# First expert layer on 256 columns of x with the weights held, for pairs of tiles of one expert

## The chip, the cores and the metric

The kernel runs on one core of a Trainium2 chip. The metric is the device time of one execution in microseconds. Engines work side by side, each through its own instructions in order: TensorE (PE in the profile, its weight loads PEld), VectorE (DVE), ScalarE (ACT), GpSimd (POOL) and SyncE (SP), which issues transfers. PSUM is the memory that TensorE writes; SBUF holds everything else.

## What is computed

Chunked attention gives x, 4608 rows (8 x 576) of 512 numbers. Each row is then sent to one of eight experts, and the expert's two layers give the output row:

```python
out = np.matmul(attn, v_c)                     # chunks of 64 rows; scores with max and exp before
x = out.transpose(0, 2, 1, 3).reshape(B, S, H * D)
logits = np.einsum('bsd,de->bse', x, w_gate)
local_gate = 1.0 / (1.0 + np.exp(-np.einsum('bsd,de->bse', x, w_local).squeeze(-1)))
for b in range(B):
    prev_e = -1
    for s in range(S):
        fresh_e = int(np.argmax(logits[b, s]))
        if s == 0 or local_gate[b, s] < 0.5:
            e = fresh_e
        else:
            e = prev_e if prev_e >= 0 else fresh_e
        prev_e = e
        ...
        h = np.maximum(x[b, s] @ w1[e], 0.0)
        out[b, s] = p[e] * (h @ w2[e])
```

w1[e] is 512 x 1024, w2[e] is 1024 x 512. The experts get very different numbers of rows, and which row goes where is known only on the chip.

## The kernel before, in words

The first 200 us are attention and routing; the rest is the expert loop. The routed rows are sorted by expert in half tiles of 64 rows. Two half tiles make a tile of 128 rows; there are 46 tile places and 38 tiles in use. A tile whose halves have two experts is *mixed*. Tiles 0 to 2 are worked beside the end of attention, by an order written out by hand (the table `PAR["drain"]`: `x0` is the transposes of tile 0's x, `m0` its first layer, `h0` the splitting of its h, `y0` its second layer, `g` a gather). From tile 3 (`EARLY`) on, `step(t, ok, mix)` writes one tile; from tile 36 (`TMIN`) on it also asks whether the tile is in use. All this stands under a manual schedule: each engine keeps the order of the code.

Products are made in three passes, since each operand is split in a high part and a low part (the number format fp32r): high by high, high by low, low by high (`PASSES`). `mm1` is the first layer: x stationary, 512 columns of W1 moving, 24 matmuls a tile, into h with the rows on partitions. So h has to be transposed for the second layer: ScalarE's Relu brings it to `hsb` (L680), eight TensorE transposes (L588) put it into PSUM again, ScalarE casts the high part (L590) and VectorE subtracts for the low part (L591). `mm2` is the second layer, 24 matmuls; `emit_y` scales by the probability and scatters the rows by an indirect transfer on GpSimd.

Order in `step(t)`, on each engine: first layer of t (L627), its probabilities (`probs`, on VectorE with one exponential on ScalarE) and Relu; the gather of tile t + 2 (L594); `next_x(t + 1)`: four transposes of x with cast and low part; `refill(0, t)`; second layer of t - 1 (L641) and its output (L699, L700); `refill(1, t - 1)`; transposes and parts of h of tile t.

`refill(which, t)` loads nothing unless the expert changes behind tile t (a register from `regs`). Then it splits the raw weights that wait in SBUF into the parts that the matmuls read, four chunks: ScalarE casts all four (L96), the low parts (L97) go to VectorE for chunks 0, 2 and 3 and to GpSimd for chunk 1; then SyncE fetches the next expert's raw weights (L868 for W1, L871 for W2). W1 must not be overwritten before the last first layer that reads it is through.

A mixed tile takes its upper 64 rows from the raw weights of the next expert, in plain fp32 (`mm1_upper` L635, `mm2_upper` L647); `rejoin` on GpSimd adds high and low parts for that. `either` is the branch between both forms; a branch is decided on each engine by a register that it has loaded.

The buffers that matter: h stands in one PSUM tile of two banks (`new_h`), y in one (`new_y`), and three PSUM tiles `tr` serve all transposes. `slots` works out the row numbers of the tiles from 8 on; its pieces stand in the first steps of the loop.

Of the kernel before, what the change touches and what calls it, by code (L numbers as in the profile page):

```python
# [24 lines left out]
P = 128  # L25
# [26 lines left out]
    ),  # L52
    "p0": "AVPA",
# [12 lines left out]
def tile_attention_then_moe(ctx: ExitStack, tc, q, k, v, wg, wl, w1, w2, out):  # L66
# [557 lines left out]
    def mm1(xs, hs, c):  # L624
        for n, (a, w) in enumerate(PASSES):
            for j in range(2):
                nc.tensor.matmul(hs[:, j], xs[a][:, c], W1[w][c][:, 512 * j:512 * j + 512],  # L627
                                 start=(c == 0 and n == 0), stop=(c == 3 and n == 2))

    def mm1_upper(xf, hm):
        for c in range(4):
            for j in range(2):
                nc.tensor.matmul(hm[HT * j:HT * j + HT], xf[:, c], raw1[c][:, 512 * j:512 * j + 512],  # L635
                                 start=(c == 0), stop=(c == 3))

    def mm2(hx, y, c):
        for f in (2 * c, 2 * c + 1):
            for n, (a, w) in enumerate(PASSES):  # L640
                nc.tensor.matmul(y, hx[f // 4][a][:, f % 4], W2[w][c][:, f % 2, :],  # L641
                                 start=(f == 0 and n == 0), stop=(f == 7 and n == 2))
# [28 lines left out]
    def new_m():  # L671
        return ps_l.tile([P, 512], F32, name="m", tag="lg")
# [130 lines left out]
    def gather_full(t):  # L803
        xgs[t] = gather(t, pc.tile([P, XR], F32, name="xg", bufs=4), x_d)
# [1 line left out]

    te8 = pc.tile([P, NTILE, E], F32, name="te8", bufs=1)
    tb8 = pc.tile([1, NTILE, E], F32, name="tb8", bufs=1)
    regs = pc.tile([1, 4, NTILE], I32, name="regs", bufs=1)
# [69 lines left out]
    @contextmanager  # L879
    def when(v):  # L880
        if v is None:
            yield
        else:
            with tc.If(v != 0):  # L884
                yield

    def step(t, ok, mix):
        tail = t >= TMIN
        if t < NTILE:
            hs, hsb = new_h()  # L890
            hm = new_m()
            with when(ok[t]):
                plain = lambda: [mm1(xps[t], hs, c) for c in range(4)]
                either(mix[t], plain, lambda: (plain(), mm1_upper(full[0, t], hm)))
# [4 lines left out]
        if t + 2 < NTILE:  # L899
            ok[t + 2] = oks[t + 2] if t + 2 in oks else valid(t + 2)  # L900
            with when(ok[t + 1]):
                gather_full(t + 2)
        if t + 1 < NTILE:
            next_x(t + 1, mix)
        y, ym = (new_y(), new_m()) if t > EARLY else (None, None)

        def down(cs):
            def plain():
                for c in cs:
                    mm2(hps[t - 1], y, c)  # L910

            either(mix[t - 1], plain, lambda: (plain(), mm2_upper(full[1, t - 1], ym) if cs[-1] == 3 else None))
            if cs[-1] == 3:
                emit_y(t - 1, y, prc[t - 1], mix[t - 1], ym)

        def next_h(g):
            hps.setdefault(t, []).append(h_parts(hsb, g, tail and t != TMIN + 2))

        if tail and t < NTILE:
            with tc.If(ok[t] != 0) as cmp:  # L920
                down((0, 1))
                next_h(0)
                down((2, 3))
            with cmp.Else():
                with when(ok[t - 1]):
                    down((0, 1, 2, 3))
        elif t > EARLY:
            with when(ok[t - 1]):
                down((0, 1, 2, 3))
        if t < NTILE:  # L930
            refill(1, t - 1)
            with when(ok[t]):
# [4 lines left out]
    def next_x(t, mix):  # L937
        mix[t] = mixs[t] if t in mixs else mixed(t)
        if EARLY < t <= TMIN:
            xps[t] = x_parts(xgs[t], t == TMIN)  # L940
        full[0, t] = rejoin(mix[t], *xps[t], "x")
        refill(0, t - 1)

    def valid(t):
        return reg(2, t, 1, [ET.PE, ET.Activation, ET.DVE, ET.Pool, ET.SP]) if t >= TMIN else None

    with tc.manual_schedule(engines=MAN | {ET.SP, ET.Pool}):
        mix, ok = {}, {EARLY: None, EARLY + 1: None}
        oks, mixs = {}, {}
        next_x(EARLY, mix)  # L950
        for t in range(EARLY, TMIN + 3):
            step(t, ok, mix)
            n = t - EARLY
            if 20 <= t < 26:
                oks[t + 16] = valid(t + 16)
                mixs[t + 16] = mixed(t + 16)
            run(sl[n:n + 1])
        with when(ok[TMIN + 2]):
            for t in range(TMIN + 3, NTILE + 1):
                step(t, ok, mix)  # L960

# [20 lines left out]
```

## Time and profile before

| | |
|---|---|
| time, median of 3 runs | 727.39 us (725.78 to 731.74) |
| profiled execution | 728.72 us, span of its instructions 726.9 us |
| tiles in use | 38 (38 scatters of y) |
| VectorE, ScalarE, GpSimd busy | 50%, 37%, 26% of the span |
| weight reloads in the loop | 28 of W1 chunks, 28 of W2 chunks (seven changes of expert) |
| DMA queues | 42.1% and 8.2% of 16 engines' span |

A row of a timeline gives the start in us, the length in us, engine, line, operation, out<-in and the number of instructions merged; in brackets how long the engine was idle before and what ended it. Matmuls are pipelined: the length of one covers its way through the array, and the next starts earlier, so rates are read from starts. A row of a group gives the count, then busy time and mean length in ns, then idle time before. In the rows of the 40 slices a digit is the busy share in tenths.

### The profile page before, as it was taken

The page shows a single profiled execution, that of the slowest core. Times are in us where ns is not written, and L with a number is a line of the kernel's source. Part 1 is how long each engine was busy: PE and PEld are TensorE (multiplying, and loading weights), DVE is VectorE, ACT ScalarE, POOL GpSimd, SP SyncE. Part 2 cuts the span into 40 slices and gives each one's busy share as a digit, 9 for nine tenths or more (in the row PEclk, how much of TensorE's full clock was granted, in tenths as well). Part 3 has the DMA queues.
Part 4 walks back from the last instruction along what each step waited for, and adds up shares of the span by engine and source line. Part 5 has one row for each costly group of instructions (what it writes and reads, how often), then busy time and mean ns, then how long its engine had stood idle before and what let it go on. Part 6 is the DMA issues. An engine that isn't in the chain of part 4 may idle for free. (4 is left out here: it accounts for less than half of the span.)

```text
span 726.9 us, 17103 instructions
## 1 busy us (share of the span) xinstructions
PE 661.4 (91%) x5594; PEld 524.8 (72%) x5594; DVE 362.0 (50%) x852; ACT 272.2 (37%) x432; POOL 188.1 (26%) x230
## 2 busy tenths in 40 slices
PE   4779898777999999999999999999999999999971
PEld 4668676565777788777888887778877888777861
DVE  2547655574685585256232562572576323454310
ACT  3547665554521234341222443422454222432210
POOL 3322233345022132123121231331243212231100
PEclk9989999998999999999999999999999999999986
DMA  9999999996833144145111253441277111333100
GB/s 211 201 200 234 233 240 245 247 254 178 217 102 118 46 148 135 71 146 164 42 46 46 84 164 101 148 156 47 79 239 249 60 44 46 97 111 130 49 19 15
DMA packets 102928, 97.49 MB, mean 134 GB/s; under 512 B 42672, under 2 KB 79536, under 8 KB 102768
## 3 DMA queue, kind: packets, MB, share of 16 engines
q1 hardware_dynamic: 96608, 75.70, 42.1%
q0 software_dynamic: 6160, 19.85, 8.2%
q8 instruction: 78, 1.28, 0.8%
q14 instruction: 82, 0.67, 0.3%
HBM read 76.48 MB, written 19.56 MB: 132 GB/s over the span
## 5 line engine op out<-in xcount | busy, mean ns | idle before, releaser
L641 PE MATMUL y<-w2h,hp 128*128 128x512 f32 x608 | 203.7, 405 | 10.3 <-DVE hp L591 6.3
L627 PE MATMUL h<-w1h,xp 128*128 128x512 f32 x608 | 178.3, 403 | 0.0
L641 PEld LDWEIGHTS y<-w2h,hp 128*128 128x128 f32 x608 | 114.9, 190 | 39.1 <-DVE hp L591 8.9
L627 PEld LDWEIGHTS h<-w1h,xp 128*128 128x128 f32 x608 | 111.4, 189 | 23.9 <-ACTq L863 0.2
L641 PE MATMUL y<-w2l,hp 128*128 128x512 f32 x304 | 121.1, 399 | 0.0
L700 POOL DMA_INDIRECT out<-ysb,sidx x38 | 41.2, 1085 | 273.5 <-DVEq L863 197.4
L627 PE MATMUL h<-w1l,xp 128*128 128x512 f32 x304 | 95.9, 396 | 0.0
L590 ACT CAST hp<-tr 128x512 fp32r<-128x512 f32 x76 | 41.2, 589 | 108.0 <-PE tr L588 97.0
L591 DVE TENSOR_TENSOR xp<-tr,xp 128x512 fp32r<-128x512 f32 x39 | 27.0, 691 | 106.5 <-ACTq L863 67.0
L699 DVE TENSOR_SCALAR ysb<-y,ppr 128x512 f32<-128x512 f32 x35 | 26.2, 747 | 92.7 <-PE y L641 81.7
L627 PEld LDWEIGHTS h<-w1l,xp 128*128 128x128 f32 x304 | 57.0, 188 | 14.7 <-DVEq L863 0.7
L641 PEld LDWEIGHTS y<-w2l,hp 128*128 128x128 f32 x304 | 57.9, 190 | 12.3
L680 ACT ACTIVATE hsb<-h 128x1024 f32<-128x1024 f32 x35 | 35.9, 1027 | 67.5 <-PE h L627 64.9
L591 DVE TENSOR_TENSOR hp<-tr,hp 128x512 fp32r<-128x512 f32 x76 | 49.2, 685 | 13.5 <-ACT hp L590 12.5
L613 ACT ACTIVATE pex<-pex 128x8 f32<-128x8 f32 x38 | 7.9, 209 | 117.2 <-DVE pex L612 117.2
L594 POOL DMA_INDIRECT xg<-x_d,gidx x36 | 36.9, 1026 | 40.7 <-issue 19.3
L97 POOL TENSOR_TENSOR w1l<-raw,w1h 128x512 fp32r<-128x512 f32 (+1 forms) x15 | 27.7, 1844 | 70.6 <-ACT w1h L96 70.6
L242 PE MATMUL o<-v,pT 64*64 64x65 f32 x1152 | 32.0, 235 | 13.5 <-DMA v<-in_v 12.9
L242 PEld LDWEIGHTS o<-v,pT 64*64 64x64 f32 x1152 | 24.6, 143 | 23.0 <-DMA v<-in_v 15.8
L588 PE MATMUL tr<-ident,hsb 128*128 128x128 f32 x304 | 40.3, 273 | 0.3 <-ACT hsb L680 0.3
L97 DVE TENSOR_TENSOR w2l<-raw,w2h 128x1024 fp32r<-128x1024 f32 x21 | 39.9, 1952 | 0.9 <-issue 0.9
L588 PEld LDWEIGHTS tr<-ident,hsb 128*128 128x128 f32 x304 | 35.3, 141 | 6.8 <-ACT w2h L96 1.2
(173 smaller groups left out, 832.5 us busy)
## 6 DMA issues: line engine op xcount, KB each, us to landing
raw<-in_moe_w SPq DMA_DIRECT2D x72, 512.0 KB, 5.0
x_d<-xs SPq DMA_DIRECT2D x18, 521.0 KB, 5.7
v<-in_v SPq DMA_DIRECT2D x72, 128.0 KB, 6.0
qt<-in_q SPq DMA_DIRECT2D x11, 512.0 KB, 6.4
kt<-in_k SPq DMA_DIRECT2D x11, 512.0 KB, 7.6
qt<-in_q SPq DMA_DIRECT2D x6, 256.0 KB, 6.2
kt<-in_k SPq DMA_DIRECT2D x6, 256.0 KB, 6.7
qt<-in_q SPq DMA_DIRECT2D x4, 384.0 KB, 7.0
```

What stands on the lines that cost most here:

```text
L97: (lo_eng or nc.vector).tensor_tensor(lo, raw, hi.bitcast(F32), ALU.subtract)
L242: nc.tensor.matmul(o[64 * cp:64 * cp + 64, cc, DV * h:DV * h + D + 1], pT[64 * cc:64 * cc + 64, 4 * j + h, 64 * cp:64 * cp + 64], vt[64 * ...
L588: nc.tensor.transpose(ps[:, n], src_of(n), ident)
L590: return [tr, lambda: nc.scalar.copy(hi, box["ps"]), lambda: V.tensor_tensor(lo, box["ps"], hi.bitcast(F32), ALU.subtract)]
L591: lambda: V.tensor_tensor(lo, box["ps"], hi.bitcast(F32), ALU.subtract)]
L594: nc.gpsimd.indirect_dma_start(out=dst, out_offset=None, in_=src, in_offset=bass.IndirectOffsetOnAxis(ap=gidx[t].bitcast(U32), axis=0))
L613: lambda: nc.scalar.activation(ex[:, 0], ex[:, 0], AF.Exp),
L627: nc.tensor.matmul(hs[:, j], xs[a][:, c], W1[w][c][:, 512 * j:512 * j + 512], start=(c == 0 and n == 0), stop=(c == 3 and n == 2))
L641: nc.tensor.matmul(y, hx[f // 4][a][:, f % 4], W2[w][c][:, f % 2, :], start=(f == 0 and n == 0), stop=(f == 7 and n == 2))
L680: nc.scalar.activation(hsb, hs.rearrange("p j f -> p (j f)"), AF.Relu)
L699: either(mix, lambda: V.tensor_scalar(ysb, y, pr, None, ALU.mult), lambda: y_mixed(ysb, y, ym, pr))
L700: nc.gpsimd.indirect_dma_start(out=out, out_offset=bass.IndirectOffsetOnAxis(ap=sidx[t].bitcast(U32), axis=0), in_=ysb, in_offset=None, bo ...
```

## The change

In the loop the tiles 4 to 35 are taken in 16 pairs (4, 5), (6, 7) and so on, by a new function `pair`. A new register, made by one more VectorE compare, says whether the first half of tile t and the second half of tile t + 1 have the same expert; since the halves are sorted, all four then have it.

If they have, the first layer is `mm1_pair`: blocks of 128 x 128 of W1 are stationary and x of both tiles moves, 256 columns, so that h comes out with its features on partitions. It is called twice, for features 0 to 511 and 512 to 1023, 48 matmuls each. ScalarE's Relu writes the high part straight from PSUM and VectorE the low part (`relu_pair`); the transposes of h, `hsb` and both casts are left out. Otherwise both tiles are worked as before, inside the pair's order. The second layer is the same.

The order in `pair(t)`: first layer of t (or features 0 to 511 of both tiles), second layer of t - 1, transposes and parts of h of t if the tiles are single; `refill(0, t)`; first layer of t + 1 (or the other features of both), gathers for the pair after the next, x of the next two tiles with `refill(0, t + 1)` behind it; second layer of t, parts of h of t + 1 if single. The high and low parts of x of both tiles lie in `xhi` and `xlo`, those of h in three buffers taken in turn (`SLOTS`), which attention used before. Three tiles instead of two are gathered in the drain.

```diff
+    def mm1_pair(xs, hT, g):
+        for f in range(4):
+            for c in range(4):
+                for n, (a, w) in enumerate(PASSES):
+                    nc.tensor.matmul(hT[:, f], W1[w][c][:, P * (4 * g + f):P * (4 * g + f) + P], xs[a][:, c],
+                                     start=(c == 0 and n == 0), stop=(c == 3 and n == 2))
+    def relu_pair(hp, hT):
+        nc.scalar.activation(hp[0], hT, AF.Relu)
+        V.scalar_tensor_tensor(hp[1], hT, 0.0, hp[0].bitcast(F32), ALU.max, ALU.subtract)
...
-        lambda: V.tensor_tensor(regs[:, 3], te[0:1, 0:NTILE], tb, ALU.not_equal),
+        lambda: (V.tensor_tensor(regs[:, 3], te[0:1, 0:NTILE], tb, ALU.not_equal),
+                 V.tensor_tensor(regs[:, 4, 0:NTILE - 1], te[0:1, 0:NTILE - 1], tb[:, 1:NTILE], ALU.is_equal)),
...
-        g=lambda: [lambda t=t: gather_full(t) for t in (EARLY, EARLY + 1)],
+        g=lambda: [lambda t=t: gather_full(t) for t in (EARLY, EARLY + 1, EARLY + 2)],
...
+    def next_xs(t, mix):
+        xp2[t] = (pc.tile([P, 4, 256], F32R, name="xhi", tag="xp", bufs=1),
+                  pa2.tile([P, 4, 256], F32R, name="xlo", tag="xs", bufs=3))
+        for d in range(2):
+            xps[t + d] = [x[:, :, P * d:P * d + P] for x in xp2[t]]
+            hilo(lambda n, d=d: xgs[t + d][:, P * n:P * n + P], *xps[t + d])
+            mix[t + d] = mixs[t + d] if t + d in mixs else mixed(t + d)
+            full[0, t + d] = rejoin(mix[t + d], *xps[t + d], "x")
+        one[t] = reg(4, t, 1, [ET.PE, ET.Activation, ET.DVE])
         refill(0, t - 1)
...
+    def pair(t, ok, mix):
+        hp = []
+        def first(d):
+            hs, hsb = new_h()
+            hm = new_m()
+            hT = hs.rearrange("p j (f t) -> p (j f) t", t=256)
+            with tc.If(one[t] != 0) as cmp:
+                mm1_pair(xp2[t], hT, d)
+            with cmp.Else():
+                up(t + d, mix, hs, hm)
+            if d == 0:
+                hp.append(new_parts())
+            with tc.If(one[t] != 0) as cmp:
+                relu_pair(hp[d], hT)
+            with cmp.Else():
+                either(mix[t + d], lambda: relu(hsb, hs), lambda: relu_mixed(hsb, hs, hm))
+            prc[t + d] = probs(xgs[t + d], ehot[:, t + d])
+            return hsb
+        def second(d, hsb):
+            y, ym = new_y(), new_m()
+            down(t + d - 1, mix, y, ym, (0, 1, 2, 3))
+            refill(1, t + d - 1)
+            if t == EARLY + 1 and d == 0:
+                run(sl[2:])
...
+            with tc.If(one[t] == 0):
+                for g in range(2):
+                    hilo(lambda n, g=g: hsb[:, 512 * g + P * n:512 * g + P * n + P], *hps[t + d][g])
+            full[1, t + d] = [rejoin(mix[t + d], *hps[t + d][g], g) for g in range(2)]
+        hsb = first(0)
+        second(0, hsb)
+        refill(0, t)
+        hsb = first(1)
+        if t + 4 < TMIN:
+            for n in (t + 4, t + 5):
+                gather_full(n)
...
+        if t + 2 < TMIN:
+            next_xs(t + 2, mix)
...
+        second(1, hsb)
...
-        for t in range(EARLY, TMIN + 3):
+        run(sl[0:1])
+        step(EARLY, ok, mix)
+        run(sl[1:2])
+        for t in range(EARLY + 1, TMIN, 2):
+            pair(t, ok, mix)
...
+        for t in range(TMIN, TMIN + 3):
             step(t, ok, mix)
```

`up` is the first layer of one tile with its mixed form, `down` the second layer with its output, as they stood in `step`.

What the instructions of a tile look like on TensorE, from the transposes of h (`hsb`) of one tile to the first layer of the next, before:

```order
L588 MATMUL tr<-ident,hsb 128x128 x7
L863 UNCONDITIONAL_BRANCH
L588 MATMUL tr<-ident,hsb 128x128
L856 COMPARE_AND_BRANCH
L856 UNCONDITIONAL_BRANCH x2
L856 COMPARE_AND_BRANCH
L856 UNCONDITIONAL_BRANCH x2
L660 COMPARE_AND_BRANCH
L627 MATMUL h<-w1h_70,xp 128x512 x2
L627 MATMUL h<-w1l_74,xp 128x512 x2
L627 MATMUL h<-w1h_70,xp 128x512 x2
L627 MATMUL h<-w1h_71,xp 128x512 x2
```

And in the changed kernel, at the same place of a pair (w1h and w1l are the parts of W1 with the chunk's number behind, xhi and xlo those of x):

```order
L1018 COMPARE_AND_BRANCH
L588 MATMUL tr<-ident,hsb 128x128 x8
L1018 UNCONDITIONAL_BRANCH x2
L869 COMPARE_AND_BRANCH
L869 UNCONDITIONAL_BRANCH x2
L869 COMPARE_AND_BRANCH
L869 UNCONDITIONAL_BRANCH x2
L876 UNCONDITIONAL_BRANCH
L995 COMPARE_AND_BRANCH
L635 MATMUL h<-xhi,w1h_70 128x256
L635 MATMUL h<-xhi,w1l_74 128x256
L635 MATMUL h<-xlo,w1h_70 128x256
```

The transposes of h now stand under a branch of their own (L1018), and the first layer changes its weights' chunk after three matmuls instead of six.

ScalarE around `refill(0, t)`, before: Relu, cast of x, then the branch and the four casts of W1, all ahead of the casts of h.

```order
L680 ACTIVATE hsb<-h 128x1024
L660 UNCONDITIONAL_BRANCH
L850 TENSOR_LOAD regs
L590 CAST xp<-tr 128x512
L856 COMPARE_AND_BRANCH
L856 UNCONDITIONAL_BRANCH x2
L850 TENSOR_LOAD regs
L863 COMPARE_AND_BRANCH
L96 CAST w1h_70<-raw_0_86 128x1024
L96 CAST w1h_71<-raw_1_87 128x1024
L96 CAST w1h_72<-raw_2_88 128x1024
L96 CAST w1h_73<-raw_3_89 128x1024
```

And now, for the change of expert between the two tiles of a pair (hhi is the high part of h):

```order
L590 CAST hhi<-tr 128x4x128 x2
L1018 UNCONDITIONAL_BRANCH x2
L869 COMPARE_AND_BRANCH
L869 UNCONDITIONAL_BRANCH x2
L869 COMPARE_AND_BRANCH
L869 UNCONDITIONAL_BRANCH x2
L863 TENSOR_LOAD regs
L876 COMPARE_AND_BRANCH
L96 CAST w1h_70<-raw_0_86 128x1024
L96 CAST w1h_71<-raw_1_87 128x1024
L96 CAST w1h_72<-raw_2_88 128x1024
L96 CAST w1h_73<-raw_3_89 128x1024
```

The casts of W1 have moved behind the two casts of h. The refill behind a pair's second tile keeps its old place, behind the casts of x.

TensorE at the entry to the loop, before: half of tile 2's second layer (y), then tile 3's first layer; the other half comes later.

```order
L641 MATMUL y<-w2h_79,hp_3667 128x512 x2
L641 MATMUL y<-w2l_83,hp_3667 128x512
L856 COMPARE_AND_BRANCH
L856 UNCONDITIONAL_BRANCH x2
L863 UNCONDITIONAL_BRANCH
L660 COMPARE_AND_BRANCH
L627 MATMUL h<-w1h_70,xp 128x512 x2
L627 MATMUL h<-w1l_74,xp 128x512 x2
```

And in the changed kernel:

```order
L649 MATMUL y<-w2h_81,hp_3671 128x512
L649 MATMUL y<-w2l_85,hp_3671 128x512
L649 MATMUL y<-w2h_81,hp_3671 128x512 x2
L649 MATMUL y<-w2l_85,hp_3671 128x512
L649 MATMUL y<-w2h_81,hp_3671 128x512
L668 COMPARE_AND_BRANCH
L627 MATMUL h<-w1h_70,xp 128x512 x2
L627 MATMUL h<-w1l_74,xp 128x512 x2
```

All of tile 2's second layer now stands ahead of tile 3's first layer.

More of the change, by code (lines that the diff above doesn't have):

```diff
@@ L808, in tile_attention_then_moe @@
     tb8 = pc.tile([1, NTILE, E], F32, name="tb8", bufs=1)
-    regs = pc.tile([1, 4, NTILE], I32, name="regs", bufs=1)
+    regs = pc.tile([1, 5, NTILE], I32, name="regs", bufs=1)
     te = pc.tile([P, NTILE + 1], F32, name="te", bufs=1)
@@ L885, in when, with up, down, plain @@
                 yield
+    def up(t, mix, hs, hm):
+        plain = lambda: [mm1(xps[t], hs, c) for c in range(4)]
+        either(mix[t], plain, lambda: (plain(), mm1_upper(full[0, t], hm)))
+    def down(t, mix, y, ym, cs):
+        def plain():
+            for c in cs:
+                mm2(hps[t], y, c)
+        either(mix[t], plain, lambda: (plain(), mm2_upper(full[1, t], ym) if cs[-1] == 3 else None))
+        if cs[-1] == 3:
+            emit_y(t, y, prc[t], mix[t], ym)
     def step(t, ok, mix):
@@ L891, in step @@
             hm = new_m()
-            with when(ok[t]):
-                plain = lambda: [mm1(xps[t], hs, c) for c in range(4)]
-                either(mix[t], plain, lambda: (plain(), mm1_upper(full[0, t], hm)))
+            with when(ok(t)):
+                up(t, mix, hs, hm)
                 prc[t] = probs(xgs[t], ehot[:, t])
@@ L898, in step @@
                     xps[t + 1] = x_parts(xgs[t + 1], t != TMIN + 2)
-        if t + 2 < NTILE:
-            ok[t + 2] = oks[t + 2] if t + 2 in oks else valid(t + 2)
-            with when(ok[t + 1]):
+        if tail and t + 2 < NTILE:
+            ok(t + 2)
+            with when(ok(t + 1)):
                 gather_full(t + 2)
-        if t + 1 < NTILE:
+        if tail and t + 1 < NTILE:
             next_x(t + 1, mix)
[L905 to L914, printed above, removed]
+        if t == EARLY:
+            next_xs(t + 1, mix)
+            for n in (t + 3, t + 4):
+                gather_full(n)
+        y, ym = (new_y(), new_m()) if tail else (None, None)
         def next_h(g):
-            hps.setdefault(t, []).append(h_parts(hsb, g, tail and t != TMIN + 2))
+            hps.setdefault(t, []).append(h_parts(hsb, g, not tail or t != TMIN + 2))
         if tail and t < NTILE:
-            with tc.If(ok[t] != 0) as cmp:
-                down((0, 1))
+            with tc.If(ok(t) != 0) as cmp:
+                down(t - 1, mix, y, ym, (0, 1))
                 next_h(0)
-                down((2, 3))
+                down(t - 1, mix, y, ym, (2, 3))
             with cmp.Else():
[L925 to L929, printed above, removed]
+                with when(ok(t - 1)):
+                    down(t - 1, mix, y, ym, (0, 1, 2, 3))
+        elif tail:
+            with when(ok(t - 1)):
+                down(t - 1, mix, y, ym, (0, 1, 2, 3))
         if t < NTILE:
             refill(1, t - 1)
-            with when(ok[t]):
+            with when(ok(t)):
                 for g in range(len(hps.get(t, ())), 2):
@@ L935, in step, with next_x @@
             full[1, t] = [rejoin(mix[t], *hps[t][g], g) for g in range(2)]
-    def next_x(t, mix):
+    def next_x(t, mix, parts=True):
         mix[t] = mixs[t] if t in mixs else mixed(t)
-        if EARLY < t <= TMIN:
-            xps[t] = x_parts(xgs[t], t == TMIN)
+        if t == TMIN:
+            xps[t] = x_parts(xgs[t], True)
         full[0, t] = rejoin(mix[t], *xps[t], "x")
-        refill(0, t - 1)
+        if t > EARLY + 1:
+            refill(0, t - 1)
+    def next_xs(t, mix):
[7 more added lines that the diff above has]
+        one[t] = reg(4, t, 1, [ET.PE, ET.Activation, ET.DVE])
+        refill(0, t - 1)
@@ new lines, in tile_attention_then_moe, with new_parts @@
+    SLOTS = ((pa2, "xT", "hp0", pc), (pa1, "v1", "hp1", pc), (pa1, "v0", "pr", pa2))
+    def new_parts():
+        n = len(made) % 3
+        made.append(n)
+        hi, thi, tlo, lo = SLOTS[n]
+        return (hi.tile([P, 4, 256], F32R, name="hhi", tag=thi, bufs=1),
+                lo.tile([P, 4, 256], F32R, name="hlo", tag=tlo, bufs=2 if tlo == "pr" else 1))
+    def pair(t, ok, mix):
[22 more added lines that the diff above has]
+                run(sl[2:])
+            if d == 0:
+                hp.append(new_parts())
+                for n in range(2):
+                    hps[t + n] = [[x[:, :, P * n:P * n + P] for x in h] for h in hp]
+            with tc.If(one[t] == 0):
[8 more added lines that the diff above has]
+            for n in (t + 4, t + 5):
+                gather_full(n)
+        elif t + 4 == TMIN:
+            gather_full(TMIN)
+            with when(ok(TMIN)):
+                gather_full(TMIN + 1)
+        if t + 2 < TMIN:
+            next_xs(t + 2, mix)
+        else:
+            ok(TMIN + 1)
+            next_x(TMIN, mix)
+        second(1, hsb)
@@ L947, in tile_attention_then_moe, with ok @@
     with tc.manual_schedule(engines=MAN | {ET.SP, ET.Pool}):
-        mix, ok = {}, {EARLY: None, EARLY + 1: None}
-        oks, mixs = {}, {}
-        next_x(EARLY, mix)
-        for t in range(EARLY, TMIN + 3):
-            step(t, ok, mix)
[L953 to L958, printed above, removed]
+        mix, oks, mixs, xp2, one, made = {}, {}, {}, {}, {}, []
+        def ok(t):
+            if t < TMIN:
+                return None
+            if t not in oks:
+                oks[t] = valid(t)
+            return oks[t]
+        mix[EARLY] = mixed(EARLY)
+        full[0, EARLY] = rejoin(mix[EARLY], *xps[EARLY], "x")
+        refill(0, EARLY - 1)
+        run(sl[0:1])
[3 more added lines that the diff above has]
+            pair(t, ok, mix)
+            if 20 <= t < 26:
+                for n in (t + 16, t + 17):
+                    ok(n)
+                    mixs[n] = mixed(n)
+        for t in range(TMIN, TMIN + 3):
+            step(t, ok, mix)
+        with when(ok(TMIN + 2)):
             for t in range(TMIN + 3, NTILE + 1):
```

2 rows, old and new, of the table PAR are left out of this document.

## The prediction

> **What bounds the kernel now.** I read the page first, then the timeline of TensorE inside one tile, then the timelines of ScalarE, VectorE and GpSimd around one weight change. On the page the busy line of PE and its slices show where the time is.
>
> ```profile
> PE 661.4 (91%) x5594; PEld 524.8 (72%) x5594; DVE 362.0 (50%) x852; ACT 272.2 (37%) x432; POOL 188.1 (26%) x230
> PE   4779898777999999999999999999999999999971
> L627 PE MATMUL h<-w1h,xp 128*128 128x512 f32 x608 | 178.3, 403 | 0.0
> L627 PE MATMUL h<-w1l,xp 128*128 128x512 f32 x304 | 95.9, 396 | 0.0
> ```
>
> From the twelfth slice on PE never rests; that is the expert loop, and no other engine is near it. The first layer has 608 + 304 = 912 matmuls for 38 tiles, 24 each. The profiled durations overlap, so a busy sum can't price them; distances between starts can. One tile on PE:
>
> ```profile
> 402.31 1.04 PE L588 MATMUL tr<-ident,hsb 128*128 128x128 f32 x8
> 403.10 0.72 PE L627 MATMUL h<-w1h,xp 128*128 128x512 f32 x2
> ...
> 408.81 0.60 PE L588 MATMUL tr<-ident,xg 128*128 128x128 f32 x4
> 409.17 0.48 PE L641 MATMUL y<-w2h,hp 128*128 128x512 f32 x1
> ...
> 414.85 1.04 PE L588 MATMUL tr<-ident,hsb 128*128 128x128 f32 x8
> ```
>
> A tile takes 414.85 - 402.31 = 12.54 us, without a gap: 0.79 for eight transposes of h, 5.71 for 24 first-layer matmuls, 0.36 for four transposes of x, 5.68 for 24 second-layer matmuls. A 512-column matmul costs about 5.62 / 24 = 0.234 us (0.07 of each block is its first weight load), a transpose 0.109. Whatever PE saves or waits goes to the end time one for one.
>
> **Which pairs take the new path.** The branch asks whether all four half tiles of a pair have one expert. Where the expert changes, SyncE reloads W1; where it changes inside a tile, that tile has the mixed matmuls.
>
> ```profile
> 230.63 0.63 PE L627 MATMUL h<-w1h,xp 128*128 128x512 f32 x2
> ```
>
> ```profile
> 263.68 4.81 SPq L868 DMA_DIRECT2D raw<-in_moe_w  x4
> ...
> 308.39 4.80 SPq L868 DMA_DIRECT2D raw<-in_moe_w  x4
> ...
> 412.94 4.83 SPq L868 DMA_DIRECT2D raw<-in_moe_w  x4
> ...
> 455.47 4.81 SPq L868 DMA_DIRECT2D raw<-in_moe_w  x4
> ...
> 522.40 17.35 SPq L868 DMA_DIRECT2D raw<-in_moe_w  x8
> ...
> 629.65 4.77 SPq L868 DMA_DIRECT2D raw<-in_moe_w  x4
> ```
>
> ```profile
> L635 PE MATMUL m<-raw,fullx x48: 592/592/643, 299.4 to 623.7; 128*64 128x512 f32 x48
> ```
>
> Tile 3 starts at 230.63, so the first reload falls after the first layer of tile 5. Counting 12.54 us a tile, the others fall after tiles 8, 16, 19, 24 and 25 (the row of eight) and 32. The 48 mixed matmuls are 16 for each of three tiles: 8, 19 and 32. Of the 16 pairs (4,5) to (34,35), five are broken: 8, 16, 18, 24 and 32 by their first tile. Eleven take the new path.
>
> **The price of a 256-column matmul.** For such a pair 2 x 24 matmuls of 512 columns become 96 of 256: as many columns, twice as many instructions, each with a weight load. Before has no such matmul in this number format; the rows around it:
>
> ```profile
> 396.60 0.19 PEld L641 LDWEIGHTS y<-w2h,hp 128*128 128x128 f32 x1
> 396.71 0.19 PEld L641 LDWEIGHTS y<-w2l,hp 128*128 128x128 f32 x1
> ```
>
> ```profile
> 266.23 2.53 PE L559 MATMUL tr<-qv,rh 128*128 128x152 bf16 x36
> 268.56 0.71 PE L627 MATMUL h<-w1h,xp 128*128 128x512 f32 x2
> ```
>
> ```profile
> 299.44 3.65 PE L635 MATMUL m<-raw,fullx 128*64 128x512 f32 x16
> 303.02 0.66 PE L588 MATMUL tr<-ident,xg 128*128 128x128 f32 x4
> ```
>
> ```profile
> 321.76 3.67 PE L647 MATMUL m<-raw,full 128*64 128x256 f32 x32
> 325.36 0.87 PE L588 MATMUL tr<-ident,hsb 128*128 128x128 f32 x6
> ```
>
> - Floor: after the transposes, one weight load of this format lets the next one start 396.71 - 396.60 = 0.11 us later. A matmul with its own load won't go below 0.110.
> - Proportional: 0.234 / 2 = 0.117. For it speaks the fp32 pair of rows: 16 of 512 columns took 3.58 us, 32 of 256 took 3.60.
> - A part that doesn't shrink: the bf16 chain does 36 x 152 columns in 2.33 us, 0.426 ns a column with everything in it. At that rate 512 columns take 0.218, so 0.016 of the 0.234 belongs to the matmul and not to its columns. Then 256 columns cost 0.109 + 0.016 = 0.125.
> - Ceiling: the line through the transposes (128 columns, 0.109) and the 512-column matmul gives 0.151 at 256.
>
> I take 0.125: the load is as large as before while the columns are half, so whatever it costs its matmul stays. The ends for the range are 0.110 and 0.151.
>
> The Trainium skill, "TensorE: Matmul & The Clock Gate", section "Back-to-back issue gap", gives N / 2.4 + 2.5 ns for a warm matmul, an estimate of 109 ns for 256 columns; by it the change would end at the floor's time below. The same rule gives 216 ns for 512 columns, where this trace has 234, so the trace doesn't agree at the size that it does show.
>
> **The change, part by part.**
>
> 1. *One-expert pairs.* Two tiles cost 2 x 12.54 = 25.08 us now. After: 96 x 0.125 = 12.00, two second layers 11.30, eight transposes of x 0.87; 24.17 in all. The sixteen transposes of h are gone (1.74 with their first loads), the smaller matmuls give half of that back. Gain 0.91 x 11 = 10.0 us. ScalarE's Relu now writes the high part itself and one VectorE instruction the low part; they lie under the second layer (5.68 us) or under the transposes of x and half of a second layer, and need about 2.5 us. If that cover went, PE would wait for the low part of h.
>
> 2. *W1 refills inside a pair* (after tiles 8, 16, 24, 32). Before, ScalarE's casts of the new W1 stand right behind the cast of x, ahead of the second layer. In the new order they stand behind the two casts of h, which wait for transposes that follow the second layer. The rows of one tile before:
>
> ```profile
> 403.04 1.07 ACT L590 CAST hp<-tr 128x512 fp32r<-128x512 f32 x2 [4.97 <-PE tr L588]
> ...
> 404.86 0.15 DVE L611 TENSOR_REDUCE pm<-xg 128x1 f32<-128x8 f32 x1
> ...
> 406.38 0.16 DVE L618 TENSOR_TENSOR ppr<-psm,pm 128x1 f32<-128x1 f32 x1
> ...
> 409.10 1.03 ACT L680 ACTIVATE hsb<-h 128x1024 f32<-128x1024 f32 x1 [3.58 <-PE h L627]
> 410.02 0.58 ACT L590 CAST xp<-tr 128x512 fp32r<-128x512 f32 x1
> 410.49 3.90 ACT L96 CAST w1h<-raw 128x1024 fp32r<-128x1024 f32 x4
> 410.63 0.69 DVE L591 TENSOR_TENSOR xp<-tr,xp 128x512 fp32r<-128x512 f32 x1 [4.09 <-ACT xp L590]
> 411.58 1.23 DVE L97 TENSOR_TENSOR w1l<-raw,w1h 128x1024 fp32r<-128x1024 f32 x1 [0.26 <-ACT w1h L96]
> 412.58 2.51 POOL L97 TENSOR_TENSOR w1l<-raw,w1h 128x1024 fp32r<-128x1024 f32 x1 [6.04 <-ACT w1h L96]
> 413.47 3.83 DVE L97 TENSOR_TENSOR w1l<-raw,w1h 128x1024 fp32r<-128x1024 f32 x2 [0.66 <-ACT w1h L96]
> ```
>
> The four low parts are there 2.3, 4.6, about 5.6 and 6.8 us after the first cast starts. Count from the end of the tile's first layer. PE: second layer to 5.68, transposes of h to 6.47, next first layer. ScalarE: casts of h begin 0.73 after the transposes (403.04 - 402.31), so 6.41 to 7.48, and W1 casts from 7.5. High part 0 comes at 8.5, the low parts at 9.8, 12.1, 13.1 and 14.3. PE starts at 8.5, waits for low part 0 until 9.8 with two matmuls done, reaches low part 1 at 11.3 and waits to 12.1; the rest arrives in time, and the layer ends at 15.9 instead of 12.2. That is 3.7 us, four times: 14.8. Before, all this was hidden (casts 1.7 us after the layer's end).
>
> 3. *W1 refills ahead of a new-path pair* (after 5, 19, 25). The order keeps the early place, but the pair's first 12 matmuls use all four chunks within 1.5 us, where a tile took them over 5.6. After tile 5, itself on the new path, ScalarE does Relu, then the exponential of the probabilities, which now waits for VectorE's low part of h, then two casts of x: W1 casts from about 4.4, low part 3 at about 11.1. PE arrives at 0.87 + 5.65 = 6.5 and would be past it at 8.0; wait 3.3. After tile 25 (Relu, exponential and two casts of x, no wait between) the W1 casts start at 2.5, and PE, with transposes of h still to do, arrives at 7.35: wait 0.7. After mixed tile 19, with its three Relu pieces, they start at 3.6: wait 1.8. Sum 5.8.
>
> 4. *W2 refills.* After tile 19 the second layer waits today:
>
> ```profile
> 479.34 0.48 PE L641 MATMUL y<-w2h,hp 128*128 128x512 f32 x1
> 486.70 0.49 PE L588 MATMUL tr<-ident,hsb 128*128 128x128 f32 x3
> ```
>
> 7.36 us against 5.68, for h's low part behind three splits on VectorE. Tile 20 will have no such step: -1.7. The waits at tiles 9, 25 and 33 stay.
>
> 5. *Entry to the loop.*
>
> ```profile
> 236.31 0.62 PE L641 MATMUL y<-w2h,hp 128*128 128x512 f32 x2
> ...
> 240.79 0.73 PE L627 MATMUL h<-w1h,xp 128*128 128x512 f32 x2
> ```
>
> Tile 3's first layer runs from 230.63, in the row above, to 236.31. From its end to the next first layer 4.5 us pass, 3.0 of them matmuls of tile 2. In the new order those stand ahead, so Relu, two casts of x and two low parts lie open: about 1.0 + 0.2 + 1.2 + 0.8 plus hand-overs, 3.1, with 1.7 of transposes under it. Cost 1.3 (bounds 0 and 3).
>
> 6. *Small things at nothing.* One more compare (0.2 us) on VectorE, a register and a branch per pair on three engines, and gathers that are issued up to a pair earlier on GpSimd, which was idle three quarters of the span. If the gathers came late, the transposes of x would wait. The broken pairs are else as before, the tail too.
>
> Sum: -10.0 + 14.8 + 5.8 - 1.7 + 1.3 = +10.2 us. The profiled execution took 728.72; that gives 738.9. It lies 1.3 above the median of 727.39, so on the median 737.6, called 738.
>
> **The rivals.**
>
> - *Floor.* Each matmul goes at its weight load, 0.110: a pair saves 25.08 - 10.56 - 12.17 = 2.35, eleven 25.9, against 20.2 of the other terms: 722, not slower. It decides from 0.1153 down. For it: the load row. Against it: 512 columns take more than their streaming and their load explains.
> - *Proportional.* 0.117: 18.5 saved, 729. The fp32 rows speak for it, another format with half-width weights.
> - *Refills hidden.* If term 2 doesn't show, because the splits come earlier than their place in the order says: 738 - 15 = 723. Against it: the two casts of h can't precede their transposes, and each engine takes its work in order.
> - *Ceiling.* 0.151: the pair costs 26.67, 1.59 more than now; 17.5 + 20.2 makes 765. The transposes' row speaks for it, though in them the columns may go at another rate.
> - *No new path.* If the branch never took it: terms 2 (refills inside a pair) and 5 alone, 743.
>
> **How the numbers follow.** Forecast (0.125, refills exposed) 0.45, proportional 0.25, floor 0.08, refills hidden 0.10, ceiling 0.09, no new path 0.03. A measurement of this kernel tells about 1% from no change, so 720 to 735 is the same. The forecast lies above that with 0.40 and inside with 0.05; the proportional case inside with 0.22, above with 0.03; ceiling and no new path above. Floor and hidden refills hold 0.18: 0.08 inside, 0.10 below, since both together, or hidden refills at 0.117 (714), pass the bound. Faster 0.10, same 0.35, slower 0.55. The range from 721 to 751 leaves out that 0.10 below and most of the ceiling above; the forecast's own range is 732 to 745.
>
> **What would show it.** The distance between starts of 256-column matmuls in a pair: 0.125 against 0.110, 0.117 or 0.151. No transposes of h in eleven pairs: 304 - 176 = 128 left. In tiles 9, 17, 25 and 33 a first layer of 9.4 us instead of 5.7, with PE idle for w1h and w1l. A wait of about 3 us ahead of tile 6. The forecast is wrong if the W1 casts start sooner than 7 us after a tile's first layer, or if PE waits inside one-expert pairs for h or x.

## The result and the profile after

The changed kernel takes 831.79 us, the median of 3 runs (830.71 to 839.76), against 727.39: a ratio of 1.145, 95% interval 1.132 to 1.159. It is slower, as was forecast, but by 104 us and not by 10. The profiled execution took 830.71, with a span of 828.8.

The busy line of TensorE (PE), its slices and its granted clock (in tenths of full speed) on the page of the changed kernel:

```profile
PE 680.2 (82%) x5946; PEld 552.6 (67%) x5946; DVE 358.3 (43%) x831; ACT 248.7 (30%) x388; POOL 191.6 (23%) x230
PE   4889878689998858989888898588795989888982
PEclk9889999989999989899999999799897999989997
```

Before, PE stood at 9 from the eleventh slice to the third from the end; now full slices are rare, and the clock dips in several. The loop has filled with holes, also where no expert changes. Two timelines of one pair without a weight change show them: first the end of a second layer (L649) and the start of a new first layer (L635), then the second half of the same pair, with VectorE's output row.

```profile
383.26 0.40 PE L649 MATMUL y<-w2h,hlo 128*128 128x512 f32 x1
...
384.62 0.36 PE L635 MATMUL h<-xhi,w1h 128*128 128x256 f32 x1 [0.96 <-PEq L1018]
```

```profile
390.19 0.28 PE L635 MATMUL h<-xlo,w1h 128*128 128x256 f32 x1
...
396.13 0.75 DVE L711 TENSOR_SCALAR ysb<-y,ppr 128x512 f32<-128x512 f32 x1 [1.60 <-PEq L1018]
...
396.99 0.36 PE L635 MATMUL h<-xhi,w1h 128*128 128x256 f32 x1 [0.96 <-DVEq L876]
...
398.38 0.39 PE L635 MATMUL h<-xhi,w1l 128*128 128x256 f32 x1 [1.03 <-DVEq L876]
```

Three things are to be seen.

- From 384.62 to 390.19 stand 48 matmuls of 256 columns, 47 distances in 5.57 us: 0.1185 each. The new first layer itself is as cheap as the proportional rival had it.
- Ahead of it 1.36 us pass between two starts where 0.23 would do, and the profile names PE's own sequencer (PEq, what runs an engine's branches, register loads and waits) at L1018, the branch that skips the transposes of h.
- In the second half of the pair the first layer's second matmul, the first that reads w1l, starts 1.39 us after its first (396.99 to 398.38) and not 0.12, waiting for VectorE's sequencer at L876. L876 is the branch around the refill; no refill is taken here. VectorE can pass that branch only after ysb (396.13 to 396.88), which waits for the second layer to end; between ysb and the end of that branch, at 398.3, it runs nothing but branches and two register loads.

The view of TensorE's waits from 234 to 770 us (line, who ended the wait, sum, times, longest) says how often:

```profile
PE h L635 <- DVEq L876: 31.7, 19, 6.8
PE h L627 <- ACT w1h L96: 9.1, 4, 2.3
PE y L649 <- issue: 8.4, 11, 1.0
PE h L635 <- ACTq L876: 7.9, 3, 3.0
PE h L627 <- issue: 7.8, 4, 3.8
PE y L649 <- DVE hlo L591: 5.5, 4, 1.8
PE h L635 <- PEq L1018: 4.1, 4, 1.1
```

And windows of the changed kernel, with the granted clock behind POOL's column, show what follows a hole:

```profile
255.00:258.00 3.00, 2.66 (x38) 2.35 (x36) 0.97 (x2) 0.00 (x0) 1.01 (x1) 1.00 0.02 7
258.00:261.00 3.00, 0.76 (x4) 0.60 (x5) 0.94 (x6) 0.00 (x0) 0.96 (x1) 0.98 0.21 81
261.00:264.00 3.00, 3.00 (x16) 3.00 (x16) 0.00 (x0) 0.00 (x0) 0.00 (x0) 0.50 0.30 92
264.00:267.50 3.50, 3.50 (x30) 3.50 (x30) 0.00 (x0) 0.00 (x0) 0.00 (x0) 0.96 0.02 5
...
384.60:390.30 5.70, 5.68 (x48) 5.70 (x49) 0.00 (x0) 0.00 (x0) 1.00 (x1) 1.00 0.13 49
```

TensorE works 0.76 us out of the three from 258 to 261, and in the next three the clock is 0.50: 16 matmuls where the price of 0.118 us would give 25.

I added up, from 234 us on, what the distances between starts on TensorE take above their price at full clock (0.118, 0.234 or 0.109 us):

| where | places | us |
|---|---|---|
| second layer to first layer (skip at L1018, whatever else ends it) | 19 | 31.7 |
| first to second matmul of the new first layer, VectorE at L876 | 12 | 28.2 |
| transposes of x to second layer ("issue") | 11 | 10.2 |
| W1 refills that are taken, high and low parts | 18 | 19.5 |
| W2 refills, as before | 4 | 6.1 |
| other matmuls that start while the granted clock is 0.50 | 196 | 23.9 |

That is 119.6. Take off 9.5 that before had too (6.7 for W2 refills, 2.8 at a lower clock) and about 17 for eleven cheaper pairs, and 93 us are left, against 101.9 between the two spans; the other 9 are single waits and small differences that the table leaves out. The 31.7 us in 19 places of the first row are not those of the first line of the view above: that line joins the 12 places at w1l with 7 of the skip.

The 12 places at VectorE's L876 are of two kinds. In nine of them, 11.7 us, VectorE has no refill at hand. In three, at 298, 531 and 638 us, 16.5 us, the block of W1 isn't taken, but VectorE comes to it late because three splits of a W2 refill, which is taken, stand ahead.

### The profile page after: what moved, and what is told of

The parts are those of the page before. It is cut to its first block, busy times and chain, and to the rows that moved or that the text cites. A ratio compares the mean times of both kernels' runs of the same rounds, so it can differ in the third digit from the quotient of the medians.

```text
span 828.8 us, 18166 instructions
## 1 busy us (share of the span) xinstructions
PE 680.2 (82%) x5946; PEld 552.6 (67%) x5946; DVE 358.3 (43%) x831; ACT 248.7 (30%) x388; POOL 191.6 (23%) x230
## 5 line engine op out<-in xcount | busy, mean ns | idle before, releaser
L635 PE MATMUL h<-xhi,w1l 128*128 128x256 f32 x352 | 107.5, 305 | 29.2 <-DVEq L876 25.0
L635 PE MATMUL h<-xhi,w1h 128*128 128x256 f32 x352 | 107.1, 304 | 24.1 <-ACTq L876 7.9
L649 PE MATMUL y<-w2h,hhi 128*128 128x512 f32 x256 | 103.1, 403 | 8.4 <-issue 8.4
L649 PE MATMUL y<-w2h,hlo 128*128 128x512 f32 x256 | 100.9, 394 | 5.5 <-DVE hlo L591 5.5
L635 PE MATMUL h<-xlo,w1h 128*128 128x256 f32 x352 | 105.4, 299 | 0.0
L649 PE MATMUL y<-w2l,hhi 128*128 128x512 f32 x256 | 100.9, 394 | 0.0
L635 PEld LDWEIGHTS h<-xhi,w1l 128*128 128x128 f32 x352 | 73.4, 209 | 33.3 <-DVEq L876 27.5
L635 PEld LDWEIGHTS h<-xhi,w1h 128*128 128x128 f32 x352 | 73.2, 208 | 31.3 <-issue 20.3
L635 PEld LDWEIGHTS h<-xlo,w1h 128*128 128x128 f32 x352 | 73.2, 208 | 0.0
L649 PEld LDWEIGHTS y<-w2h,hhi 128*128 128x128 f32 x256 | 48.0, 188 | 22.7 <-issue 12.9
L649 PEld LDWEIGHTS y<-w2h,hlo 128*128 128x128 f32 x256 | 48.1, 188 | 18.5 <-DVE hlo L591 7.2
L649 PEld LDWEIGHTS y<-w2l,hhi 128*128 128x128 f32 x256 | 48.1, 188 | 9.7
L242 PE MATMUL o<-v,pT 64*64 64x65 f32 x1152 | 33.5, 236 | 14.5 <-DMA v<-in_v 11.7
```

The lines of the kernel that those rows point to most:

```text
L242: nc.tensor.matmul(o[64 * cp:64 * cp + 64, cc, DV * h:DV * h + D + 1], pT[64 * cc:64 * cc + 64, 4 * j + h, 64 * cp:64 * cp + 64], vt[64 * ...
L635: nc.tensor.matmul(hT[:, f], W1[w][c][:, P * (4 * g + f):P * (4 * g + f) + P], xs[a][:, c], start=(c == 0 and n == 0), stop=(c == 3 and n ...
```

## The experiments

Theory at the start: the new layer is fine; three hand-overs around it ("branch" at L1018, the refill's place at L876, the registers that are loaded on TensorE ahead of the second layer) leave TensorE idle, and the idle time costs clock on top. Rival: the taken refills, my own forecast, weigh far more than I thought. The first four runs change one hand-over each, then all three.

**The refill ahead of the second layer**

```diff
         hsb = first(0)
+        refill(0, t)
         second(0, hsb)
-        refill(0, t)
```

> The refill of W1 behind a pair's first tile stands ahead of the second layer of the tile before, as it did before the change, on every engine; nothing else differs from the changed kernel. Theory (the place of that refill is the largest loss): the second matmul of a pair's second half waited for VectorE to pass the refill, taken or not, in 12 places 28.2 us in all, and the four taken refills cost about 14 us more, and each wait of over 3 us was followed by matmuls at a granted clock of 0.50. All of that goes: 831 becomes 780 to 790, the waits of line 635 for VectorE's line 876 fall below 8 us. Rival (PE waits there for VectorE's work on h or x, whatever stands between): time within 8 us of 831 and the waits remain under another name.

767.71 in one run, 64 us less than the changed kernel and less than I expected. The waits at the first w1l fell from 28.2 to 0.7 us, the low clock's share from 23.9 to 5.7, and the waits for W1 refills that are taken from 19.5 to 5.2. This one place carries more than half of the loss. The edit moves taken and not-taken refills alike, so alone it doesn't tell the theory from the rival; the sums do: 27.5 us of what went stood at blocks of W1 that weren't taken, 14 at those that were. The rival has a part in the first as well, by the three W2 refills ahead.

**A matmul in the empty side of the skip**

```diff
-            with tc.If(one[t] == 0):
+            with tc.If(one[t] == 0) as cmp:
...
+            with cmp.Else():
+                nc.tensor.transpose(trp()[:, 0:P], ident, ident)
```

> In the changed kernel a pair of one expert skips the transposes of h by a branch whose other side is empty on TensorE. Here that side does one 128 x 128 transpose of the identity into a PSUM tile that nobody reads. Theory (the empty side holds a wait until TensorE has finished all earlier matmuls, about 1.1 us beyond a matmul's spacing, 22 times; with a matmul there, the count that other engines need rides on it and nothing drains): line 649 to the next 635 takes about 0.35 us instead of 1.36, total 18 to 25 us less, 806 to 813. Rival (the gap is the branches themselves, five compares of 0.05 to 0.3 us on the sequencer, or code loading): the added transpose costs 22 x 0.11, 832 to 834, and the gaps stay over 1.2 us.

817.97 in one run: 14 us less, not 18 to 25. The hand-over itself is cured, as this timeline of the run shows, with the added transpose at L1022:

```profile
393.91 0.39 PE L649 MATMUL y<-w2h,hlo 128*128 128x512 f32 x1
394.14 0.27 PE L1022 MATMUL tr<-ident 128*128 128x128 f32 x1
394.17 0.36 PE L635 MATMUL h<-xhi,w1h 128*128 128x256 f32 x1
396.65 0.39 PE L635 MATMUL h<-xhi,w1l 128*128 128x256 f32 x1 [2.12 <-DVEq L876]
```

The first layer follows at 0.26 us, and then waits 2.48 us at its second matmul, where it waited 1.39. VectorE hasn't become any slower; TensorE only comes sooner. The waits there rose from 28.2 to 36.4 us in all. At three places the first layer still waits, 8.5 us, for ScalarE's sequencer at L876; two of them are among the 19 of the skip, so some 6 of its 31.7 us are W2 refills.

**The registers of a pair loaded a pair ahead**

```diff
-            mix[t + d] = mixs[t + d] if t + d in mixs else mixed(t + d)
...
-        one[t] = reg(4, t, 1, [ET.PE, ET.Activation, ET.DVE])
...
+    def pair_regs(t, mix):
+        for d in range(2):
+            mix[t + d] = mixs[t + d] if t + d in mixs else mixed(t + d)
+        one[t] = reg(4, t, 1, [ET.PE, ET.Activation, ET.DVE])
...
             down(t + d - 1, mix, y, ym, (0, 1, 2, 3))
+            if d == 0 and t + 2 < TMIN:
+                pair_regs(t + 2, mix)
             refill(1, t + d - 1)
```

> The three registers that each pair needs (two for mixed tiles, one for the pair's branch) are loaded a pair ahead, after the second layer in the middle of the pair before, instead of between the transposes of x and the second layer. Theory (TensorE's sequencer is busy with three loads of about 0.9 us each there, and its lead of 2 us over the 256-column matmuls doesn't cover them: 0.87 us, 11 times, charged to no other engine): 821, and the last transpose of x is followed by the second layer after 0.11 us instead of 0.97. Rival (the gap is the wait for code behind a branch): 831 and the gap stays.

838.89 in one run, not 821: 7 us above the changed kernel's median, but inside the range of its three runs (830.71 to 839.76), so it isn't shown to be slower; it isn't faster. The 10.2 us between the transposes of x and the second layer are gone, but the waits at the first w1l rose from 28.2 to 35.9. The loads stand on VectorE and ScalarE as well, now ahead of the branch at L876; that they lengthen the wait there is read from the order, not tested by itself.

**All three**

> The three edits together. Theory (the three places are the loss, and the 256-column matmul at 0.118 us is a gain of 1.6 us a pair): at least 80 us of the 104 come back, 725 to 750. What is left over 727 should be the three refills ahead of a pair (about 6 us), the entry to the loop (1 to 3 us), and slow-clock stretches behind them. Rival (removing one wait only uncovers the next, on VectorE's order): over 775.

731.38, against 729.72 for the kernel before beside it: ratio 1.002, interval 0.999 to 1.006. Single edits gave -64, -14 and +7, and all three at once -100: two of the three pay fully only once the wait behind them is gone too.

**Two of the three**

> The refill moved ahead of the second layer and the matmul in the empty side, without the registers loaded early: what the three register loads cost by themselves. Theory (about 0.87 us of bare issue in each of 11 pairs, once nothing else is late): the three edits' 731 + 10 = 741. Rival (the loads only use time that TensorE would wait for VectorE anyway, as the single edit with early registers was slower than the changed kernel): 731 to 734.

739.99, ratio 1.022, interval 1.014 to 1.030 (two runs): the register loads do cost time once nothing else is late, 9 us by the two medians. TensorE's waits in this run show where:

```profile
PE y L649 <- ACT hhi L696: 7.6, 9, 1.5
```

ScalarE is named, but the high part of h was long there; the loads stand between.

**An empty skip in the kernel before**

Here the suspected cost is added to the kernel before and nothing else. The edit puts a skipped block ahead of the transposes of h:

```diff
             refill(1, t - 1)
+            if EARLY < t < TMIN:
+                with tc.If(mix[t] != 0):
+                    nc.tensor.transpose(trp()[:, 0:P], ident, ident)
```

> The kernel before with a block for TensorE in each of 30 tiles, ahead of the transposes of h, that holds one transpose and is skipped in all but the tiles of two experts. Theory (the empty side waits for all matmuls ahead of it, so the skip costs 1.1 to 1.2 us each): 727.4 + 33 = 760, more where the clock falls. Rival (a skip costs its two branches, some 0.4 us that the queue of matmuls hides): 727 to 731.

741.38 in one run, +15 us: between the two theories. The timeline at one such place:

```profile
250.26 0.39 PE L641 MATMUL y<-w2h,hp 128*128 128x512 f32 x1
250.95 1.07 PE L588 MATMUL tr<-ident,hsb 128*128 128x128 f32 x8 [0.30 <-PEq L933]
```

0.69 us between starts and not 0.23: 0.46 each, 28 times, 12.9. So the empty side does wait for all matmuls, but that costs only 0.46. In the changed kernel the same hand-over cost 1.13. There, three more compares and branches follow the skip on TensorE's sequencer (two at L869, one at L995) and here none does. That made a new theory: the wait takes away the cover under which the next branches run.

**The same skip with branches behind it**

The same block, moved behind the transposes of h, where two branches and a compare follow.

> The kernel before with the same skipped block as in the earlier run, but behind the transposes of h, where two branches of the GpSimd sums and the compare of the first layer follow it on TensorE's sequencer. Theory (after the empty side has waited for all matmuls, the branches that follow can no longer run beside matmuls, so each adds its 0.2 to 0.27 us): about 1.0 us in each of 28 tiles, 726.5 + 28 = 754. Rival (only the wait itself costs, the 0.46 us a tile of the earlier run): 740 to 742.

773.50 in one run, +48 us. One tile, and one of six in which the loop also loads two registers for later tiles at this place:

```profile
382.96 1.04 PE L588 MATMUL tr<-ident,hsb 128*128 128x128 f32 x8
385.08 0.70 PE L627 MATMUL h<-w1h,xp 128*128 128x512 f32 x2 [1.09 <-ACT hp L590]
```

```profile
486.41 1.09 PE L588 MATMUL tr<-ident,hsb 128*128 128x128 f32 x8
489.90 0.71 PE L627 MATMUL h<-w1h,xp 128*128 128x512 f32 x2 [2.40 <-issue]
```

From the transposes to the first layer 2.12 us pass, 0.79 before the edit: 1.33 more, and at six tiles 2.4 to 2.7 more. TensorE's sequencer shows how: at the first of the two tiles its wait for the matmuls ends at 384.09, three compares of 0.207 us follow, 0.265 apart, and only then the first layer starts. All of these holes together, by distances, are 44.5 us. The theory holds with a larger price than I gave it, because whatever stands on the sequencer behind the wait is laid open: register loads too. Four stretches at a lower clock come on top, about 1.5 us each, one of them after the wait that ended at 489.90 (0.50 between 492 and 494 us); the waits for W2 that before had, 6.7 us, are swallowed by the new ones.

```profile
490.00:492.00 2.00, 2.00 (x7) 1.59 (x8) 2.00 (x2) 0.00 (x0) 2.00 (x1) 0.72 0.51 100
492.00:494.00 2.00, 2.00 (x7) 1.52 (x6) 2.00 (x2) 0.00 (x0) 0.44 (x1) 0.50 0.75 257
```

**Splits on VectorE alone**

What was left in the version with all three edits pointed at VectorE's splits of refilled weights. Their row there, and in the kernel before (minimum, median and longest in ns):

```profile
L97 DVE TENSOR_TENSOR w2l<-raw,w2h x21: 1207/1225/3423, 285.7 to 659.1; 128x1024 fp32r<-128x1024 f32 x21
```

```profile
L97 DVE TENSOR_TENSOR w2l<-raw,w2h x21: 1206/1217/3425, 281.2 to 653.7; 128x1024 fp32r<-128x1024 f32 x21
```

Most take 1.22 us, some 3.42. GpSimd splits the second of the four chunks at the same time. So the edit is to take GpSimd out:

```diff
-                split(hi[c], lo[c], raw[c], nc.gpsimd if c == 1 else nc.vector)
+                split(hi[c], lo[c], raw[c], nc.vector)
```

> The three edits together, and each refill's second chunk split on VectorE instead of GpSimd. Theory (what is left of the waits comes from splits that GpSimd and VectorE do side by side: in the run of the three edits one VectorE split of each refill took up to 3.42 us where the others took 1.2, so four on VectorE alone need 4.9 us and end about 1.8 us earlier): the waits for the low halves of the second layer (6.1 us), for the second transposes of x (5.0) and for GpSimd's chunk (1.8) go, and about half of the 13.6 us of halved clock behind them: 708 to 715. Rival (the slow split is slow for another reason, four take 7.8 us on VectorE): 735 to 740.

715.62, against 726.46 for the kernel before beside it: ratio 0.987, interval 0.982 to 0.992. The row in this run, and a window of it with the granted clock, 1.00, behind POOL's column:

```profile
L97 DVE TENSOR_TENSOR w2l<-raw,w2h x28: 1208/1219/1287, 283.5 to 643.1; 128x1024 fp32r<-128x1024 f32 x28
```

```profile
234.00:690.00 456.00, 444.75 (x2626) 374.25 (x2624) 204.26 (x440) 131.53 (x193) 79.46 (x77) 1.00 0.32 106
```

All 28 take 1.2 us: GpSimd's help cost VectorE up to 2.2 us per refill and saved it 1.2. TensorE's waits for the low part of h behind the splits of W2 fell from 5.5 to 1.5 us, and the lower clock went with them, all of it: 7.3 us with three edits, none here from 234 to 690 us. (The 13.6 in the expectation also counted distances at full clock that run over their price, those of mixed tiles above all.)

The same line alone in the kernel before:

> The kernel before with each refill's second chunk split on VectorE. If VectorE is held up by GpSimd's split there too, the waits for the second layer's low halves (about 6 us in all) go: 719 to 723. Rival (VectorE's longer list only moves the wait): 727 within 2 us, or slower.

720.30 against 726.46, ratio 0.991, interval 0.989 to 0.994. Here PE's wait for the low part of h behind the splits, 6.1 us in four places before, is 1.1.

**Two column groups side by side**

On top of that, the new first layer takes features in pairs of blocks, so that a chunk of W1 is needed later:

```diff
-        for f in range(4):
-            for c in range(4):
+        for f, c in [(f, c) for b in range(2) for c in range(4) for f in (b, b + 2)]:
+            if True:
```

> As the run before it, and the new first layer goes over two column groups side by side, so that a chunk of the weights is needed every 0.7 us instead of every 0.35. Theory (a refill ahead of a pair is waited for chunk by chunk, 5.3 us in three places): 2 to 3 us less than the run before it. Rival (the last chunk's arrival decides): no difference, within 0.5 us.

711.77, ratio 0.980 to the kernel before, interval 0.976 to 0.985. The waits for w1l fell from 2.1 to 0.5 us, as meant. Whether the time fell isn't settled: the median is 3.9 us below that of the splits on VectorE, but the two intervals overlap and the profiled spans are 711.2 and 711.0. This version, with all five edits, has the lowest median, and the interval of its ratio to the kernel before lies below 1. Three rows of TensorE in it:

```profile
375.75 0.27 PE L1028 MATMUL tr<-ident 128*128 128x128 f32 x1
...
387.11 0.27 PE L1028 MATMUL tr<-ident 128*128 128x128 f32 x1
...
399.36 0.27 PE L1028 MATMUL tr<-ident 128*128 128x128 f32 x1
```

A pair takes 399.36 - 375.75 = 23.61 us, against 25.08 for two tiles before.

**The old path in the fastest version**

The compare that makes the flag is turned into one that is never true (`ALU.is_gt`), so that every pair goes as two single tiles in the same order of work.

> The fastest version so far with the flag for pairs of one expert held at 0, so that every pair takes the path of single tiles. Theory (the new first layer is worth 25.08 - 23.5 = 1.6 us in each of 11 pairs): 711.8 + 17 = 729. Rival (in that version the gain comes from the splits and the earlier refill, the new path brings less than 0.5 us a pair): 712 to 717.

727.53, against 725.52 beside it (1.003, interval 1.000 to 1.006). The new first layer is thus worth about 16 us, 1.4 in each of eleven pairs; without it the other edits of that version only pay for what the new order costs.

## Why the prediction was wrong

- **Price of a 256-column matmul** (0.125): measured 0.118, the proportional rival. The step that failed in it is the part "that doesn't shrink", taken from a chain in bf16; the fp32 rows, which I called another format, were the better guide. The Trainium skill's rule (TensorE: Matmul & The Clock Gate, "Back-to-back issue gap"), which that section gives for an isolated matmul, made it an estimated 109 ns; the trace stays above it, by 9 ns at 256 columns as by 18 at 512. By itself this is worth 9 us: at 0.117 the same sum gives the proportional rival's 729.
- **Term 1** (gain 10.0): the mechanism was right, 128 transposes of h are left as forecast. At the measured price the pair should take 96 x 0.118 + 11.30 + 0.87 = 23.5; the fastest version shows 23.61, and the run of the old path in that version makes it 1.4 us of gain a pair. In the changed kernel it was there too, and buried.
- **Term 2** (refills inside a pair, 14.8): right in place and mechanism. From the last transpose of h to the last matmul of the next first layer, by their starts, the changed kernel takes 6.0, 4.1, 5.1 and 6.4 us more than the usual 5.5 at tiles 9, 17, 25 and 33: 21.6, lower clock included, and about 14 without it. But I used the mechanism for taken W1 refills alone. The block's place on VectorE binds the other pairs as well: there the first reader of w1l waits until VectorE has passed a branch around nothing, and in three places until it has done the W2 refill ahead of that branch. That wait, 28.2 us in 12 places, is in no term.
- **Term 3** (refills ahead of a pair, 5.8 from 3.3, 1.8 and 0.7): right, 5.3 us in the version with all three edits, from 3.1, 1.7 and 0.6.
- **Term 4** (-1.7) and **term 5** (+1.3): small, as forecast. The wait after tile 19 is gone as forecast, but two of the other three grew by 0.4 us and one of 0.4 came at tile 17: 6.1 us of waits for W2 are left of 6.7. The entry costs about 1.4 in the version with all three edits (the parts written down for it add up to 3.2, not 3.1).
- **Term 6** ("small things at nothing") is the step that failed. "A register and a branch per pair on three engines" are 31.7 us at the skip, some 6 of them due to W2 refills, and 10.2 at the register loads. I named no cover for them. What had covered their like before was the queue of matmuls that TensorE works off while its sequencer runs ahead, and a skip with an empty side ends just that cover. The added skips in the kernel before show it: 0.46 us for the wait, 1.3 with branches behind it, 2.4 to 2.7 with register loads as well.
- **The clock** was in no term: 23.9 us. Each of the twelve stretches at 0.50 between 234 and 800 us begins during a hole on TensorE or within 2.4 us of its end; in the version with all three edits the share is 7.3 us, and with the splits on VectorE nothing from 234 to 690 us.
- **The rivals** all argued about the matmul's price and the taken refills, between 722 and 765. None had the control flow, so no end of the range could hold the result. The sign to watch, "PE waits inside one-expert pairs", was named, and it came, though not for h or x. That the time fell on the slower side is only in part the forecast's merit: terms 2 and 3 were there, some 27 us, but the gain of term 1 takes back 17 of that, and most of the 104 us came from what stood at nothing.

## What to carry to other kernels

Count a skip on an engine by what its empty side waits for and by what stands behind it on that sequencer, and count a conditional block as a wait at its place even where it isn't taken: put it where its engine comes early, or give the readers work to do first. When several waits lie one behind another, an edit that removes a front one can show little or nothing; try them together before judging one. And a second engine that helps is only help if the first keeps its speed.

## What the runs showed of the hardware

- **Clock after idle time.** Waits here are distances between starts. In the kernel before with skips and branches, none of 22 waits of 1.2 to 1.6 us on TensorE was followed by a lower clock within 9 us; of six waits of 2.4 to 2.7 us four were followed by a stretch at 0.50 that cost about 1.5 us each. In the kernel before, four waits of 1.8 to 2.2 us cost nothing; in the version with all three edits five of six waits of 1.8 to 2.2 us were followed by such a stretch. The Trainium skill (TensorE: Matmul & The Clock Gate, "HAM oscillation — how this bites in real kernels") speaks of idle gaps over about 3.4 us; these runs show the halving after shorter ones, if not each time.
- **VectorE beside GpSimd.** A VectorE subtraction that reads two tiles of SBUF took 3.42 us when it began beside GpSimd's like one and 1.22 without. The Trainium skill (SBUF — State Buffer, "Who interferes with whom") says that such an instruction contends with a GpSimd instruction that reads SBUF; the traces agree, and taking GpSimd away from a quarter of the splits made the kernel before 0.9% faster.
- **Branches on TensorE.** A compare with its branch takes 0.207 us there (median), 0.045 on ScalarE, as these rows of the changed kernel show; the empty side's semaphore wait is the third.

```profile
L1018 ACTq COMPARE_BRANCH  x42: 34/45/50, 253.4 to 778.0; - x42
L1018 PEldq COMPARE_BRANCH  x42: 72/207/325, 256.3 to 776.1; - x42
...
L1018 PEldq EVENT_SEMAPHORE  x22: 51/51/51, 257.8 to 779.3; - x22
```

What stays open: two of the six waits of 2.4 us or more weren't followed by a lower clock, and waits of about 2 us mostly were in one kernel and never in the other; no run here says why.
